# A new hand-written order for a cosine attention and highway FFN kernel: its first pair apart, whole-batch loads, one Newton chain per batch, and GpSimd operations marked to go ahead of VectorE

## The chip, the cores and the metric

The kernel runs on one core of one Trainium2 chip. The metric is device time in microseconds (us). Of the kernel before there are three runs: 308.99, 310.39 and 311.38 us, median 310.39. Engines are called by short names: PE (TensorE, matmuls), DVE (VectorE), ACT (ScalarE), POOL (GpSimd), SP (SyncE, which here only issues DMAs). A `q` behind a name (SPq, POOLq) is that engine's instruction queue.

## The reference, cut to what matters

```python
# q, k, v: (8, 12, 448, 64) float32; tau = 0.1; x: (3584, 768)
q_n = q / (np.linalg.norm(q, axis=-1, keepdims=True) + 1e-06)
k_n = k / (np.linalg.norm(k, axis=-1, keepdims=True) + 1e-06)
scores = np.matmul(q_n, k_n.transpose(0, 1, 3, 2)) / tau
attn = softmax(scores)                       # rows sum to 1
x = np.matmul(attn, v)                       # (8, 12, 448, 64)
x = x.transpose(0, 2, 1, 3).reshape(8 * 448, 12 * 64)
H = np.maximum(x @ w_h, 0.0)
T = 1.0 / (1.0 + np.exp(-(x @ w_t + b_t)))
out = T * H + (1.0 - T) * x                  # (3584, 768)
```

Eight batches of twelve heads: each head has 448 rows of 64. Then a two-matrix gated FFN over 3584 rows of 768.

## The kernel before, in words

**Tiling.** A batch has six *pairs*; pair p holds heads p and 6+p. The 448 rows of a head are three chunks of 128 ("main") and a tail of 64 ("tail"). With s = 6b + p, a pair goes through these steps:

- *Loads.* q and k main rows are cast to float16 by DMAs that POOL issues into `qr` and `kr` (`load_main`, L325 and on). The tails `qt` and `kt` and the values `vr` and `vt` come in float32 by DMAs that SP issues (`load_tails`, `load_v`). For batch 0, pairs 0 to 2 come in float32 into `f0` by SP (q) and ACT (k) instead (`load_first`), and its tails are spread over SP, POOL and ACT. From batch 2 on the loads are gated in the plan on an exponential of an earlier pair.
- *Norms.* Squares (L423 and L449 on ACT, L425 on DVE), two folding adds and a reduction on DVE (L440 to L442) give sums of squares `n2`. `newton` (L468 to L475) makes the reciprocal square root in seven small DVE instructions. A batch from 1 on has two such chains: tails with pairs 0 to 2 (48 columns), and pairs 3 to 5 (36 columns). Batch 0 has three: tails with pair 0, pairs 1 and 2, pairs 3 to 5.
- *Scaling.* `qn` and `kp` (L494) and the q tails `qtn` (L507) on POOL, 128x384 each, the k tails `kb` (L521) on DVE. For pair 0 of batch 0, `kp` is on DVE.
- *Turn.* Nine PE transposes into one PSUM bank (L539 to L547), copied by DVE to `qT` (L553).
- *Scores and exponentials.* Three chunks of scores (L562, two matmuls each) and one for the tails (L576); ACT takes exponentials of 128x896 into `E` (L569) and of 128x512 into `Et` (L581).
- *Attention.* 32 small PE matmuls of 65 columns (L610, L613, L629; the 65th column of the values is 1 and gives the row sum), then on DVE a reciprocal (L643) and a multiply into `x` (L646).

When a batch's six pairs are done its FFN follows, in four row tiles of 128 rows (the last one holds the 64 tail rows of two halves). The tile is transposed: for batches 1 to 6 by a DMA on SP (`xd`, L672), for batches 0 and 7 by PE and a DVE copy (L678, L683). Matmuls with `wt` and `wh` (L712, tails L707, bias L701 and L698) go to PSUM banks; ACT takes a tanh (L726), DVE makes `hm` (L733), the gate (L740) and their product (L744), POOL adds x (L750), SP stores (L758, L760). The last two tiles are added on DVE.

**What sets the order.** Nothing is scheduled at run time. Every step is recorded as an operation with an engine, reads, writes and a number in order of recording. `ORDER` lists these numbers; `pl.follow(ORDER, SLOTS)` (L814) replays them, and `SLOTS` names the buffer that each new tile takes. Each engine, and each engine's DMA queue, runs its own operations strictly in that order, waiting by semaphores for what it reads. An operation that is late therefore holds all that stand behind it on its engine. SP carries loads, transposes and stores in one queue.

[...]

The functions below are those of the kernel before, with the line numbers of its profile.

Of the kernel before, what the change touches and what calls it, by code (L numbers as in the profile page):

```python
# [15 lines left out]

ORDER = tuple(
    int(n)
    for n in """
# [83 lines left out]
22001023122030021300111011123110111101320111110002011122301023100123000200133222002110311220012011310010021300  # L103
20121013211220011301001231102110300011011021100231001120230022203001103112310222003121222130101102320103120201
22213
""".replace("\n", "")
)


# [10 lines left out]

class Plan:

    FREE = ("B", "sq", "f1", "f2")
    AHEAD = {"S": 2}
    SWITCH = 92.0
# [62 lines left out]
def pe(occ):  # L192
    return occ, occ + 205
# [665 lines left out]
```

## Time and profile before

| what | us |
|---|---|
| median of three runs | 310.39 |
| their range | 308.99 to 311.38 |
| the profiled execution, span from first to last instruction | 309.1 |
| PE busy in it | 266.1 |
| DVE busy | 236.1 |
| ACT busy | 206.4 |
| POOL busy | 149.7 |

The profile gives one execution and its span; it has no other time of its own, and the span lies between the lowest run and the median. In its rows L712 is line 712 of the kernel; `x4` is four instructions taken together; what stands in brackets is how long the engine was idle just before and what released it. Rows of stretches give, for each engine, busy us and in brackets the number of instructions, then the granted PE clock (1.00 is full), the busy share of the DMA engines and GB/s. A busy PE is not PE at its peak: a matmul's row includes its time in the pipeline.

### The profile page before, as it was taken

Reading aid. Unit: us, or ns where it says so; the run is one execution under the profiler, and the core shown is the slowest. Engines: PE = TensorE matmul, PEld = TensorE weight load, DVE = VectorE, ACT = ScalarE, POOL = GpSimd, SP = SyncE. Lnnn points to the kernel's source line nnn. Section 1 sums busy time; section 2 is a strip of 40 time slices with the busy share of each in tenths; the row PEclk is TensorE's granted clock in tenths of the full one; section 3 lists DMA queues with packets and bytes.
Section 4 is the critical chain, followed back from the end, with each engine's and each line's share of the span. In section 5 each row is a group of like instructions: output and inputs, shape, how many; then the busy total and the mean of one; then the engine's idle time right before and its main releaser. Section 6 shows DMA issues by size and latency. Waiting matters only on the chain.

```text
span 309.1 us, 7922 instructions
## 1 busy us (share of the span) xinstructions
PE 266.1 (86%) x3178; PEld 164.9 (53%) x3178; DVE 236.1 (76%) x548; ACT 206.4 (67%) x327; POOL 149.7 (48%) x162
## 2 busy tenths in 40 slices
PE   0039798999899999995699699989999999999992
PEld 0015566657565466554365556646666665656651
DVE  5798797798999659994689848996789855444574
ACT  1415799998897778761498368987498858771210
POOL 8244648416653862593432694429623780520440
PEclk9999799999999999999599899999999999999999
DMA  7999999993137794379815399714991221601223
GB/s 161 225 222 205 245 197 231 185 127 123 54 83 136 211 216 63 130 96 226 168 63 48 105 253 225 127 30 79 209 254 37 74 70 26 180 21 48 102 78 128
DMA packets 79749, 42.20 MB, mean 137 GB/s; under 512 B 60224, under 2 KB 76608, under 8 KB 79712
## 3 DMA queue, kind: packets, MB, share of 16 engines
q1 hardware_dynamic: 53104, 29.60, 40.5%
q0 software_dynamic: 24992, 11.31, 28.5%
q10 hardware_dynamic: 1616, 0.79, 1.0%
q8 instruction: 25, 0.41, 0.6%
q14 instruction: 12, 0.10, 0.1%
HBM read 37.75 MB, written 11.01 MB: 158 GB/s over the span
## 4 chain that ended last, share of the span: by engine, by line
PE 46%; DVE 22%; DMA 13%; issue 6%; SPq 5%; POOL 4%; ACT 2%; POOLq 0%; DVEq 0%; ACTq 0%
PE pB L712 20%; PE pS L562 6%; PE pB L613 5%; DMA kt<-in_k_dram 5%; DMA qr<-in_q_dram 3%; DMA qt<-in_q_dram 3%; DVE qT L553 2%; DVE sq L425 2%; PE pB L576 2%; DVE hm L733 2%; PE pB L707 2%; DVE x L646 2%; PE pB L610 2%; PE pB L629 2%; DVE n L442 2%
## 5 line engine op out<-in xcount | busy, mean ns | idle before, releaser
L569 ACT ACTIVATE E<-pS 128x896 f16<-128x896 f32 x144 | 126.5, 923 | 32.1 <-PE pS L562 31.6
L750 POOL TENSOR_TENSOR os<-x,hm 128x768 f32<-128x768 f16 (+1 forms) x30 | 44.3, 1484 | 63.7 <-DVE hm L744 45.7
L712 PEld LDWEIGHTS <-xT 128*128 128x128 f16 x576 | 52.5, 99 | 39.2 <-issue 11.3
L712 PE MATMUL pB<-wt,xT 128*128 128x384 f16 x288 | 61.5, 330 | 0.1
L712 PE MATMUL pB<-wh,xT 128*128 128x384 f16 x288 | 59.4, 328 | 0.7 <-DVE x L646 0.6
L613 PE MATMUL pB<-vp,E 128*128 128x65 f16 x864 | 49.5, 197 | 0.0
L494 POOL TENSOR_TENSOR kp<-kr,rs 128x384 f16<-128x384 f16 x45 | 37.0, 833 | 24.7 <-DVE sq L425 6.8
L562 PE MATMUL pS<-qT 64*128 64x448 f16 x288 | 45.5, 369 | 3.5 <-ACT E L569 2.3
L726 ACT ACTIVATE tt<-pB 128x384 f16<-128x384 f32 x56 | 27.7, 496 | 31.1 <-PE pB L712 26.0
L494 POOL TENSOR_TENSOR qn<-qr,rs 128x384 f16<-128x384 f16 x45 | 37.4, 843 | 19.6 <-DVE f L440 5.4
L610 PE MATMUL pB<-vp,Et 128*128 128x65 f16 x288 | 43.7, 196 | 1.5 <-DVE qT L553 0.9
L613 PEld LDWEIGHTS <-E 128*128 128x128 f16 x864 | 40.6, 100 | 4.1 <-issue 1.5
L733 DVE SCALAR_TENSOR_TENSOR hm<-pB,x 128x384 f16<-128x384 f32 x56 | 30.5, 551 | 14.8 <-PE pB L712 11.8
L581 ACT ACTIVATE Et<-pB 128x512 f16<-128x512 f32 x48 | 28.4, 605 | 14.3 <-PE pB L576 13.9
L553 DVE COPY qT<-pB 128x1024 f16<-128x1024 f16 x48 | 32.7, 685 | 5.7 <-PE pB L547 5.4
L610 PEld LDWEIGHTS <-Et 128*128 128x128 f16 x288 | 28.6, 99 | 8.7 <-issue 5.8
L646 DVE SCALAR_TENSOR_TENSOR x<-pB,rd 128x448 f16<-128x448 f32 x48 | 29.6, 621 | 0.9
L539 PE MATMUL pB<-ident,qtn 128*128 128x128 f16 x24 | 5.7, 236 | 22.9 <-POOL qtn L507 18.3
L562 PEld LDWEIGHTS <-qT 64*128 64x128 f16 x288 | 10.8, 94 | 25.1 <-issue 19.5
L643 DVE RECIPROCAL rd<-pB 128x7 f32<-128x7 f32 x48 | 9.2, 196 | 18.6 <-PE pB L613 18.2
L440 DVE TENSOR_TENSOR f<-sq 128x1152 f16<-128x1152 f16 (+2 forms) x25 | 15.6, 625 | 9.7 <-ACT sq L449 6.1
L507 POOL TENSOR_TENSOR qtn<-qt,rs 128x384 f16<-128x384 f32 x8 | 6.6, 828 | 31.8 <-DVE rs L475 27.4
(73 smaller groups left out, 453.9 us busy)
## 6 DMA issues: line engine op xcount, KB each, us to landing
vr<-in_v_dram SPq DMA_DIRECT2D x8, 1152.0 KB, 11.1
out_dram<-os SPq DMA_DIRECT2D x24, 384.0 KB, 2.7
kr<-in_k_dram POOLq DMA_DIRECT2D x7, 576.0 KB, 12.6
qr<-in_q_dram POOLq DMA_DIRECT2D x7, 576.0 KB, 9.7
vt<-in_v_dram SPq DMA_DIRECT2D x16, 96.0 KB, 8.5
out_dram<-os SPq DMA_DIRECT2D x16, 96.0 KB, 2.2
qt<-in_q_dram SPq DMA_DIRECT2D x30, 48.0 KB, 5.5
kt<-in_k_dram SPq DMA_DIRECT2D x14, 96.0 KB, 7.3
```

What stands on the lines that cost most here:

```text
L494: return e.tensor_mul(R("qn" if t == 0 else "kp", s).rearrange("l c ab d -> l ab c d"), rows(t, b, p, p + 1)[:, :, 0, :].rearrange("l ab ( ...
L553: op("DVE", f"cpT {s}", lambda: nc.vector.tensor_copy(R("qT", s)[:, :], R16(("T", ti))[:, :]), o, l, key, r=[("B", ("T", ti))], w=[("qT", s)])
L562: nc.tensor.matmul(R("S", 3 * s + c)[:, ab, 0:448], lhsT=qT[:, 512 + 128 * c : 640 + 128 * c], rhs=qT[:, 64 * (1 - ab) : 64 * (1 - ab) + 4 ...
L569: nc.scalar.activation(R("E", s)[:, c, :, 0:448], R("S", 3 * s + c)[:, :, 0:448], AF.Exp, scale=inv_tau)
L581: op("ACT", f"exp {s} t", lambda: nc.scalar.activation(R("Et", s)[:, 64:576], R("B", ("S", s))[:, :], AF.Exp, scale=inv_tau), o, l, key + 0.3,
L610: nc.tensor.matmul(U[:, 2 * c + ab, :], lhsT=Et[:, 128 + 128 * c : 256 + 128 * c], rhs=vp[:, 6 + ab, :], start=True, stop=False)
L613: nc.tensor.matmul(U[:, 2 * c + ab, :], lhsT=EF[:, j, 576 * ab + 128 * c : 576 * ab + 128 * c + 128], rhs=vp[:, 3 * ab + j, :], start=Fals ...
L646: op("DVE", f"ev {s}", lambda: nc.vector.scalar_tensor_tensor(out=R("x", b)[:, :, D * p : D * p + D], in0=U_()[:, :, 0:D], scalar=0.0, in1 ...
L712: nc.tensor.matmul(P[:, 0:MH], lhsT=xT[:, cc, :], rhs=w_[:, cc, MH * mh : MH * mh + MH], start=st, stop=(cc == CC - 1))
L726: op("ACT", f"th {g} {mh}", lambda pi=pi, mh=mh: nc.scalar.activation(R("tt", g)[:, MH * mh : MH * mh + MH], R("B", ("P", pi))[:, 0:MH], A ...
L733: nc.vector.scalar_tensor_tensor(out=R("hm", g)[:, MH * mh : MH * mh + MH], in0=R("B", ("P", pi))[:, 0:MH], scalar=0.0, in1=xs, op0=ALU.ma ...
L750: op(en, f"out {g}", lambda: eng.tensor_add(R("os", g)[:, 0:W], xall(), R("hm", g)[:, 0:W]), o, l, at + 0.1, r=[("gg", g), ("x", b)], w=[( ...
```

## The change

The arithmetic of the FFN, the scores and the attention is the same, and so are PE's 3178 matmuls that produce results. What differs:

- **First pair apart.** Only pair 0 of batch 0 comes in float32 (`f0`, q first on SP's queue, k first on ACT's). Its own tail rows are loaded apart from those of the other pairs (`load_first_tails`). `first_pair` squares them (q on DVE, k and tails on ACT), folds 15 columns, runs a Newton chain of 15 columns, and does all five scalings of the pair on DVE. Pairs 1 and 2, then 3 to 5, are loaded as float16 by POOL, in eight DMAs; their squares are all on ACT. The norm chains of batch 0 are then: pair 0; tails with pairs 1 and 2; pairs 3 to 5.
- **Whole-batch loads** from batch 1 on keep their shape, but every DMA is an operation of its own in the order (before, the DMAs of a tail or of two halves were recorded as one), and the gates are gone. The two DMAs of a tail tile's store, the clears of the buffers and the two halves of the v tail's copy are split too.
- **One Newton chain** for each of batches 2 to 7, over 84 columns (batch 1 keeps two). Newton steps and the v copies of batch 0 are now `port=True`.
- **Warm matmuls.** 20 operations of two matmuls each on a constant tile `fill`, results unused: eleven ahead of the first turn, nine later, among the pairs of batch 0.
- **Marked POOL operations.** 49 numbers in `URGENT`. In the replay a marked POOL operation makes the next DVE operation of the port wait for it, if no other POOL operation of the port stands between.
- **A new order** throughout, with new `SLOTS`.

On DVE the program has 499 rows where it had 538, on ACT 328 for 310, on SP 125 for 94 (DMAs of one line that stand together count once), on POOL 164 for 164. In the new order POOL issues the first loads, makes ten scalings of batch 0, and then issues the two weight loads; before, it issued the load of `wh` ahead of all scalings and that of `wt` among them.

The diff, cut to its core (the two tables of numbers, and steps that are only recorded apart, are left out):

```diff
+URGENT = frozenset(
+    int(n)
+    for n in """
+131 132 169 188 414 415 434 467 554 572 591 592 629 648 649 682 699 716 763 768 769 825 845 864 1003 1040 1041
+1078 1079 1112 1157 1217 1218 1237 1256 1294 1327 1361 1451 1452 1470 1542 1576 1587 1623 1628 1629 1648 1758
+""".split()
+)
...
+    fill = sb.tile([128, 384], FP16, name="fill")
+    f0 = sb.tile([128, 2, 2, NCH * D], FP32, name="first")
...
+    def warm(n, key):
+        i = fills[0]
+        fills[0] += 1
+
+        def fn():
+            for _ in range(n):
+                ins = nc.tensor.matmul(R("B", ("W", i))[:, 0:384], lhsT=fill[:, 0:128], rhs=fill[:, 0:384],
+                                       start=True, stop=True)
+            return ins
...
+    def load_first_tails(key):
+
+        for h, e, en in ((0, nc.sync, "SP"), (1, nc.sync, "SP")):
+            op(en, f"ldqa {h}", lambda h=h, e=e: e.dma_start(
+                R("qt", 0)[64 * h : 64 * h + 64, :, 0, :],
+                q[0, :, 3 * 128 : S, :].rearrange("(ab h) l d -> h l ab d", ab=2)[3 * h]), key, w=[("qt", 0, 0)])
+        for ab, e, en in ((0, nc.scalar, "ACT"), (1, nc.scalar, "ACT")):
+            op(en, f"ldka {ab}", lambda ab=ab, e=e: e.dma_start(
+                R("kt", 0)[64 * ab : 64 * ab + 64, 0, :], k[0, 6 * ab, 3 * 128 : S, :]), key + 0.01, w=[("kt", 0, 0)])
...
+    def first_pair(key):
+        def sqm(t):
+            d = sq0[:, 6 * t : 6 * t + 6, :].rearrange("l (a c) d -> l a (c d)", a=2)
+            a = f0[:, t]
+            return nc.scalar.activation(d, a, AF.Square) if t else nc.vector.tensor_mul(d, a, a)
...
+        steps("0 0", lambda: n20[:, :], lambda j: rs0[:, j, :], 15, [("n20", 0)], [("rs0", 0)], [], key + 0.1)
+        for t in range(2):
+            op("DVE", f"{'qk'[t]}n 0", lambda t=t: nc.vector.tensor_mul(
...
-            square(b, 0, 3, base - 5.0)
-            square_tail(b, base - 4.0)
-            newton(b, (6, 0, 1, 2), base - 3.9)
-            square(b, 3, 6, base - 2.5)
-            newton(b, (3, 4, 5), base - 2.4)
...
+            nb = base - (10 if b == 1 else 12)
+            square(b, 0, 3, nb)
+            square_tail(b, nb)
+            if b == 1:
+                newton(b, (6, 0, 1, 2), nb + 2)
+                square(b, 3, 6, nb + 4)
+                newton(b, (3, 4, 5), nb + 6)
             else:
+                square(b, 3, 6, nb - 3)
+                newton(b, (6, 0, 1, 2, 3, 4, 5), nb + 2)
...
-    last = None
+    last = ahead = None
     with nc.allow_low_precision(reason="fp16 operands of the products, squares and gates as given"):
         with tc.manual_schedule():
             for o in plan:
                 ins = o.fn()
                 if o.port and o.eng == "DVE":
-                    last = ins
-                elif o.port and last is not None:
-                    after(ins, last)
+                    if ahead is not None:
+                        after(ins, ahead)
+                    last, ahead = ins, None
+                elif o.port and o.eng == "POOL":
+                    if last is not None:
+                        after(ins, last)
+                    ahead = ins if o.seq in URGENT else None
```

More of the change, by code (lines that the diff above doesn't have):

```diff
@@ L276, in R16, with clear, fn @@
     def R16(i):
         return R("B", i).bitcast(FP16)
-    def clear(tiles, views):
-        def fn():
-            for t in tiles:
+    def clear(name, tiles, views, key, gap=0):
+        for n, t in enumerate(tiles):
+            def fn(t=t):
                 for vw, x in views(t):
-                    nc.vector.memset(vw, x)
-        return fn
-    def ident_():
-        make_identity(nc, ident)
+                    ins = nc.vector.memset(vw, x)
+                return ins
+            op("DVE", f"{name} {n}", fn, key + gap * n, w=[(name, n)])
@@ L304 @@
[L304 to L311 removed]
+        (t[0:64, :, 6, D : D + 1], 1.0), (t[64:128, :, 7, D : D + 1], 1.0)], 2, 22)
@@ L352, in load_tails, with fq @@
+    def load_tails(b, key):
         for h in range(2):
-            e, en = (nc.gpsimd, "POOL") if b == 0 and h == 1 else (nc.sync, "SP")
-            def fq(h=h, e=e):
-                for ab in range(2):
-                    e.dma_start(
+            for ab in range(2):
+                def fq(h=h, ab=ab):
+                    return nc.sync.dma_start(
                         R("qt", b)[64 * h : 64 * h + 64, ab],
-                        q[b, 6 * ab + 3 * h : 6 * ab + 3 * h + 3, 3 * 128 : S, :].rearrange("h l d -> l h d"),
-                    )
@@ new lines, in load_v, with weights @@
+    def load_v(b, key):
+        op("SP", f"ldv {b}", lambda: nc.sync.dma_start(R("vr", b)[:, :, :], main_src(v, b)), key, w=[("vr", b)])
+        for ab in range(2):
+            op("SP", f"ldvt {b} {ab}", lambda ab=ab: nc.sync.dma_start(
+                R("vt", b)[64 * ab : 64 * ab + 64, :, :], tail_src(v, b, ab)), key + 0.01, w=[("vt", b)])
+    def weights(key):
+        for w_src, w_dst, nm in ((moe_w_t, wt, "wt"), (moe_w_h, wh, "wh")):
+            op("POOL", f"ld {nm}", lambda w_src=w_src, w_dst=w_dst: nc.gpsimd.dma_start(
+                w_dst[:, :, :], w_src.rearrange("(cc p) m -> p cc m", p=128)), key, w=[(nm, 0)])
+        op("POOL", "ld b", lambda: nc.gpsimd.dma_start(bth[:1, :], moe_b_t), key, w=[("bth", 0)], r=[("zb", 0)])
@@ L412, in square, with fn @@
-    def square(b, p0, p1, key):
-        g0, g1 = 12 * (p0 % 3), 12 * (p0 % 3) + 12 * (p1 - p0)
-        n = 192 * 2 * (p1 - p0)
+        return ("qr" if t == 0 else "kr", b, p)
+    def square(b, p0, p1, key, engs=("DVE", "DVE")):
+        g1 = 12 * (p1 - p0)
         i = (b, p0)
-        for t in range(2):
-            onact = b == 0 and p0 < 3 and (p0 > 0 or t == 0)
-            def fn(t=t, onact=onact):
+        for t, eng in enumerate(engs):
+            def fn(t=t, eng=eng):
                 a = rows(t, b, p0, p1)
-                d = R("sq", i)[:, g0:g1, :].rearrange("l (p a c) d -> l a p (c d)", a=4, c=NCH)[:, 2 * t : 2 * t + 2]
-                if onact:
-                    nc.scalar.activation(d, a, AF.Square)
-                else:
-                    return nc.vector.tensor_mul(d, a, a)
-            o, l = act(n) if onact else dve(n, 1 if first(b, p0) else 2)
-            op("ACT" if onact else "DVE", f"sq {b} {p0} {t}", fn, o, l, key, r=[rowtok(t, b, p) for p in range(p0, p1)],
-               w=[("sq", i)], port=not onact)
-        folds(f"fold {b} {p0}", b, i, g0, g1, 12 + 12 * p0, [("n2", b, p) for p in range(p0, p1)], key)
@@ new lines, in fn, with folds, v_ @@
+                if eng == "ACT":
+                    return nc.scalar.activation(d, a, AF.Square)
+                return nc.vector.tensor_mul(d, a, a)
+            op(eng, f"sq{p1 - p0} {b} {p0} {t}", fn, key,
+               r=[rowtok(t, b, p) for p in range(p0, p1)], w=[("sq", i)], port=eng == "DVE")
+        folds(b, i, 0, g1, col(b, p0), [("n2", b, p) for p in range(p0, p1)], key)
+    def folds(b, i, g0, g1, to, done, key):
+        def v_(r):
+            return R(r, i)[:, g0:g1, :]
+        n = g1 - g0
+        w0, w1 = ("fa",) + i, ("fb",) + i
+        op("DVE", f"fa{n} {b} {i[1]}", lambda: nc.vector.tensor_add(v_("f1"), v_("sq")[:, :, 0:32], v_("sq")[:, :, 32:64]),
+           key, r=[("sq", i)], w=[w0], u=[("f1", i)], port=True)
+        op("DVE", f"fb{n} {b} {i[1]}", lambda: nc.vector.tensor_add(v_("f2"), v_("f1")[:, :, 0:16], v_("f1")[:, :, 16:32]),
+           key, r=[w0], w=[w1], u=[("f1", i), ("f2", i)], port=True)
+        op("DVE", f"fc{n} {b} {i[1]}", lambda: nc.vector.reduce_sum(R("n2", b)[:, to : to + n], v_("f2"), axis=AX.X),
+           key, r=[w1], w=done, u=[("f2", i), ("n2", b)])
@@ L463, in step, with steps @@
+    def steps(name, n2_, rs_, n, need, done, use, key):
         def step(i):
-            n2 = R("n2", b)[:, lo:hi]
-            y, t, u = (R("rs", b)[:, j, lo:hi] for j in range(3))
+            n2 = n2_()
+            y, t, u = (rs_(j) for j in range(3))
             v_ = nc.vector
             if i == 0:
-                v_.tensor_scalar(out=y.bitcast(I32), in0=n2.bitcast(I32), scalar1=-0.5,
-                                 scalar2=float(0x5F3759DF), op0=ALU.mult, op1=ALU.add)
-            elif i in (1, 4):
-                v_.tensor_mul(t, y, y)
-            elif i in (2, 5):
-                v_.scalar_tensor_tensor(out=u, in0=t, scalar=-0.5, in1=n2, op0=ALU.mult, op1=ALU.mult)
-            else:
-                v_.scalar_tensor_tensor(out=y, in0=u, scalar=1.5, in1=y, op0=ALU.add, op1=ALU.mult)
@@ new lines, in step @@
+            if i in (1, 4):
+                return v_.tensor_mul(t, y, y)
+            if i in (2, 5):
+                return v_.scalar_tensor_tensor(out=u, in0=t, scalar=-0.5, in1=n2, op0=ALU.mult, op1=ALU.mult)
+            return v_.scalar_tensor_tensor(out=y, in0=u, scalar=1.5, in1=y, op0=ALU.add, op1=ALU.mult)
+        for i in range(7):
+            op("DVE", f"nt{n} {name} {i}", lambda i=i: step(i), key + 0.001 * i,
+               r=need if i == 0 else [("nt", name, i - 1)], w=[("nt", name, i)] + (done if i == 6 else []), u=use, port=True)
@@ new lines, in ffn @@
+        rows_ = out[b * S : b * S + S]
+        if tail:
+            for h in range(2):
+                op("SP", f"sth {g} {h}", lambda h=h: nc.sync.dma_start(
+                    rows_[384:448, MH * h : MH * h + MH], R("os", g)[64 * h : 64 * h + 64, 0:MH]), at + 0.4,
+                   r=[("os", g)], w=[("o", g)])
+        else:
+            op("SP", f"st {g}", lambda: nc.sync.dma_start(
+                rows_[0:384].rearrange("(l c) m -> l c m", c=NCH)[:, i, :], R("os", g)[:, :]), at + 0.4,
+               r=[("os", g)], w=[("o", g)])
@@ new lines @@
+    OFF = 1.5
+    for b in range(B):
+        base = at_(6 * b)
+        if b == 0:
+            load_first(0)
+            load_first_tails(0.2)
+            load_main("qr", q, b, 1, 3, 1)
+            load_main("kr", k, b, 1, 3, 1.1)
+            load_main("qr", q, b, 3, 6, 4)
+            load_main("kr", k, b, 3, 6, 4.1)
+            load_v(b, 4)
+            weights(10)
+            first_pair(3)
+            square(b, 1, 3, 6, ("ACT", "ACT"))
+            square_tail(b, 6.5)
+            newton(b, (6, 1, 2), 7)
+            square(b, 3, 6, 10, ("ACT", "ACT"))
+            newton(b, (3, 4, 5), 11)
+            for n in range(20):
+                warm(2, 0.5 * n)
+        else:
+            ld = 8 if b == 1 else base - 40
+            load_main("qr", q, b, 0, 6, ld)
+            load_main("kr", k, b, 0, 6, ld + 0.1)
+            load_tails(b, ld + 4 if b == 1 else ld)
+            load_v(b, ld + 10)
+            nb = base - (10 if b == 1 else 12)
[5 more added lines that the diff above has]
+                newton(b, (3, 4, 5), nb + 6)
+            else:
+                square(b, 3, 6, nb - 3)
+                newton(b, (6, 0, 1, 2, 3, 4, 5), nb + 2)
+        qtnorm(b, base - 8 if b else 11)
+        ktnorm(b, base - 8 if b else 11)
+        vtcast(b, base - 6)
+        for p in range(NP):
+            s = 6 * b + p
+            t = at_(s)
+            if s > 0:
+                scaled(0, b, p, t - 6, "POOL")
+                scaled(1, b, p, t - 6, "POOL")
+            turn(b, p, t - 3)
+            vcast(b, p, t - 2)
+            scores(b, p, t)
+            attend(b, p, t + 3)
```

517 lines of the change are left out of this document (211 added, 306 removed), and 143 rows, old and new, of the table ORDER.

## The prediction

> **What bounds the kernel now.** I read the page first, then a table of busy time by stretch, then the timeline of the first 50 us, then the chain of waits and the DMA view.
>
> ```profile
> span 309.1 us, 7922 instructions
> ...
> PE 46%; DVE 22%; DMA 13%; issue 6%; SPq 5%; POOL 4%; ACT 2%; POOLq 0%; DVEq 0%; ACTq 0%
> ```
>
> The second line is the chain that ended last: PE holds less than half of it, so the end is set by PE with DVE steps and DMA landings between. Where PE sits still is seen in the stretches (PE busy first, then weight loads, DVE, ACT, POOL, granted clock, DMA share):
>
> ```profile
> 10.00:20.00 10.00, 1.14 (x9) 0.88 (x9) 8.56 (x26) 1.99 (x3) 3.01 (x4) 1.00 1.32 234
> 20.00:30.00 10.00, 8.01 (x64) 4.43 (x64) 8.45 (x22) 5.77 (x8) 4.98 (x6) 1.00 1.27 200
> 30.00:40.00 10.00, 7.70 (x97) 5.10 (x96) 8.10 (x21) 6.83 (x10) 6.38 (x8) 0.83 1.13 237
> 140.00:160.00 20.00, 14.54 (x176) 9.15 (x176) 11.40 (x23) 9.52 (x18) 7.92 (x9) 0.83 0.87 168
> 160.00:180.00 20.00, 17.53 (x200) 10.16 (x197) 17.01 (x42) 12.58 (x19) 9.31 (x12) 0.91 0.48 100
> 180.00:200.00 20.00, 20.00 (x250) 12.57 (x248) 16.21 (x32) 17.10 (x31) 10.97 (x11) 1.00 1.16 178
> 300.00:309.10 9.10, 3.30 (x33) 1.80 (x31) 4.93 (x10) 0.52 (x2) 0.76 (x1) 0.93 0.32 112
> ```
>
> A healthy stretch is 180 to 200: PE never idle, 250 matmuls in 20 us, or 12.5 per us. Against it stand four losses: the head (nothing before 10; 9 matmuls up to 20, 64 and 97 in the next two stretches), 5.46 us idle at 140 to 160, 2.47 at 160 to 180, and the 5.80 of the tail. The head and the middle are what the change can reach.
>
> The head, from the whole timeline and then from ACT's own:
>
> ```profile
> 3.22 1.55 POOL L334 DMA_DIRECT2D qr<-in_q_dram  x2
> ...
> 16.58 0.83 POOL L494 TENSOR_TENSOR qn<-f,rs 128x384 f16<-128x384 f32 x1 [3.24 <-DVE f L441]
> ...
> 18.26 0.29 PE L539 MATMUL pB<-ident,qtn 128*128 128x128 f16 x1 [18.26 <-POOL qtn L507]
> ```
>
> ```profile
> 21.67 0.60 ACT L581 ACTIVATE Et<-pB 128x512 f16<-128x512 f32 x1 [6.28 <-PE pB L576]
> 22.16 2.54 ACT L569 ACTIVATE E<-pS 128x896 f16<-128x896 f32 x3
> 24.57 1.06 ACT L597 CAST vp<-vt 64x384 f16<-64x384 f32 x2
> 26.83 1.96 ACT L569 ACTIVATE E<-pS 128x896 f16<-128x896 f32 x2 [1.20 <-PE pS L562]
> 30.96 0.52 ACT L449 ACTIVATE sq<-kt 128x384 f16<-128x384 f32 x1 [2.17 <-DMA kt<-in_k_dram]
> 31.39 3.32 ACT L569 ACTIVATE E<-pS 128x896 f16<-128x896 f32 x4
> ```
>
> ```profile
> 49.46 0.51 PE L678 MATMUL pB<-ident,x 128*128 128x128 f16 x6
> ```
>
> The first transposes wait for POOL, and POOL (qn, 16.58) waited 3.24 us for a fold of pairs 1 and 2 on DVE that pair 0 does not need. The first exponential comes at 21.67, and the first turn of attended rows (L678, the start of the FFN) at 49.46. Six pairs in 27.8 us is 4.6 each; ACT alone needs 3 x 0.83 + 0.60 = 3.09 for a pair.
>
> **The change part by part.** *Head.* Only pair 0 keeps the float32 path; its q goes first on SP's queue and its k first on ACT's, its 15 norm columns get a chain of their own, and its five scalings run on DVE, so the POOL wait of 3.24 is gone. But in the written order the fold and Newton steps of pairs 1 and 2 stand on DVE ahead of pair 0's tail scalings, and they read q and k of pairs 1 and 2, now loaded by POOL. The DMA view (size, median us to landing):
>
> ```profile
> wh<-in_moe_w_h_dram POOLq DMA_DIRECT2D x1, 1152.0 KB, 22.3
> wt<-in_moe_w_t_dram POOLq DMA_DIRECT2D x1, 1152.0 KB, 10.3
> f<-in_k_dram ACTq DMA_DIRECT2D x3, 192.0 KB, 5.4
> f<-in_q_dram SPq DMA_DIRECT2D x3, 192.0 KB, 6.2
> xT<-x SPq DMA_TRANSPOSE x24, 2.9
> qr<-in_q_dram POOLq DMA_DIRECT2D x2, 144.0 KB, 6.7
> kr<-in_k_dram POOLq DMA_DIRECT2D x2, 144.0 KB, 8.2
> kt<-in_k_dram ACTq DMA_DIRECT2D x2, 96.0 KB, 4.8
> ```
>
> POOL's issues take 1.55/2 = 0.78 each, so the fourth (k of pairs 1 and 2) goes at about 1.3 + 3 x 0.78 = 3.6 (estimate) and lands 8.2 later, at 11.8 (6.7 would give 10.3). ACT squares it (0.9 for 768 columns, by the 0.83 of an exponential of 896), then 14 DVE steps at 0.29 (mean of L473 below) follow: 11.8 + 0.9 + 4.1 = 16.8 for the first turn. From turn to first exponential before took 21.67 - 18.26 = 3.41, of which about 1 (estimate) is DVE doing a fold first; in the new order the copy is next on DVE, so 2.4, giving 19.2 against 21.67. From there ACT is the bound: six pairs at 3.09 = 18.5, plus 1.0 (estimate, 1152 columns) for a square of pairs 3 to 5 that moves from DVE to ACT, 2 x 0.52 for the squares of batch 1's tails and 1.06 for the v tail: 40.8, and 1.5 (estimate) for the last attention and its division: FFN starts at 42.3. Before, at 49.46, PE had also done 1.3 us of batch 1 (a turn and one pair's scores, 16 matmuls at 12.5 per us). Gain 49.46 - 1.3 - 42.3 = 5.9. I take 5.0, because the weights are now issued after ten POOL scalings, and a wait of 0.9 for them is likely. Ends: 0 (pair 0 held by loads as before) and 9 (the kt wait of 2.17, the shorter landing and faster steps on top).
>
> Of the two FFN weight loads, wh leaves POOL near 30 (ten scalings, of which the last wait for the second Newton chain), where before it went ahead of all scalings; its cover is the ACT-bound phase up to 42.3. Without it the price is under the rivals.
>
> *Forty warm matmuls.* 22 stand before turn 0, where PE did nothing, and the others between pairs that wait for ACT: cost 0, bounded by PE's idle 8.86 in 10 to 20. The gain: stretch 30 to 40 was granted 0.83, so PE was half-clocked in part; a warm clock shortens the first turn and scores by some 0.6. I take 0: the fills start when pair 0's q has landed and end near 12 (estimate), some 5 us before the turn. [...]
>
> *Loads on POOL's queue.* Eight pieces of batch 0 now go there. The row at 3.22 shows 0.78 for each issue beside a busy DVE. [...]
>
> *Later batches: loads.* What failed at 140 to 160, from the chain of waits:
>
> ```profile
> 137.36 0.71 SPq L357
> 138.11 8.47 DMA qt<-in_q_dram
> ```
>
> ```profile
> SPq L760 <- POOL os L750: 73.9, 18, 11.4
> ```
>
> The q tails were issued late on SP (behind stores that wait for POOL, second fence, 73.9 us in all), took 8.47 to land, ACT stood at the square, and DVE, POOL and PE after it. 8.47 us is 106 matmuls. In the order of before, of the tail loads of batches 2 to 7, 14 have fewer than 100 matmuls between issue and first reader (16 the fewest, those of the failing batch 37 to 61); in the new order 4 (61, 73, 76, 80). Of 5.46 idle I take 5.0 as gone (0.46 is ordinary). What is late next: k tails of batch 6 (61 matmuls, 4.9 us), which at a quiet landing is enough. Ends: 0 and 6.5 (the clock of 0.83 there too).
>
> *One Newton chain* for batches 2 to 7: 6 x 7 = 42 DVE instructions go; the others do 84 columns at about the same price.
>
> ```profile
> L471 DVE TENSOR_TENSOR rs<-rs 128x36 f32<-128x36 f32 (+2 forms) x34 | 13.5, 396 | 0.5
> L475 DVE SCALAR_TENSOR_TENSOR rs<-rs 128x36 f32<-128x36 f32 (+2 forms) x34 | 12.7, 374 | 0.6
> ...
> L473 DVE SCALAR_TENSOR_TENSOR rs<-rs,n 128x36 f32<-128x36 f32 (+2 forms) x34 | 9.9, 290 | 0.5
> ```
>
> Each chain has two of each and a seed: 2 x (0.396 + 0.374 + 0.290) = 2.12, times 6 = 12.7 us of DVE. With DVE at 22% of the chain, 2.8 of it is on the path. Ends 0 (all hidden) and 6 (half; the dip at 160 to 180, where DVE is busy 17 of 20, is such a place). Against it: all of batch b's pairs now wait for the later squares too; cover: in the new order the last Newton step stands some 5 us of PE's matmuls or more ahead of the first turn of its batch.
>
> [...]
>
> *New order, transposes by DMA.* They land in 2.9 (row above), 36 matmuls. With fewer than 50 matmuls ahead there were 2 of 24; now there are 9 (24 to 43). Three are short of 36, by up to 1 us each: 1.0 in all. Ends 0 and the rival below. PE's useful matmuls, the exponentials and the last tile on DVE are the same: tail 0.
>
> Sum against the profiled execution: 309.1 - 5.0 - 5.0 - 2.8 + 0.5 + 1.0 = 297.8. The median of the runs, 310.39, stands 1.3 above that execution, so **299.1**.
>
> **The rivals.** (1) *Slower: transposes take the place of the tail loads.*
>
> ```profile
> DMA to landing us min/median/max: 2.3/2.9/8.6
> ```
>
> Nine tiles have 24 to 43 matmuls, about 2.8 us, between issue and reader, and PE takes its work in order. Landing can be 8.6. If these nine land at a mean of 4.7 us, each stops PE for 1.8: 299.1 - 1.0 + 16.2 = 314.3. It decides (above 313.5) from a mean of 4.6. For it: SP carries loads, stores and transposes in one queue. Against: the median.
>
> (2) *The weights are late.* wt goes at about 29 (estimate: the second Newton chain ends near 24, and six scalings of 0.83 follow) and wh a little later. Landing like wt before (10.3) wt is there at 39, and PE does not wait; like wh before (22.3) it is there at 51 against 42.3, and PE, in order, waits 9. I take 5 between them: 304. For it: ten POOL scalings stand ahead. Against: when wh was issued before, most of the first loads were still outstanding.
>
> (3) *More is gained.* Landing 6.7 (-1.5), DVE steps at 0.2 (14 x -0.09, -1.3), Newton at half (-3.2), no transposes late (-1.0): 292.
>
> (4) The DVE time and the earlier head do not reach the end, because POOL and ACT take the place: only the stall goes, 299.1 + 5.0 + 2.8 = 306.9; I count it with (2).
>
> **How the numbers follow.** Forecast as summed 0.52 (own range 295 to 304), rival 1 0.20, rivals 2 and 4 0.15, rival 3 0.13. Within 1% (307.3 to 313.5, about what a measurement here can tell from no change) falls 0.02 of the forecast, 0.05 of rivals 2 and 4, 0.02 of rival 1; slower 0.18 of rival 1 and 0.01 of the rest; faster 0.72. The range 288 to 313 takes in the rest, with the end of the head's bound below rival 3, and leaves out most of rival 1.
>
> **What would show it.** Head: first exponential near 19.2, first transpose of attended rows near 42.3; wrong if the exponential is after 21.5 or PE waits for wt. Stall: no ACT wait over 3 us on a qt or kt DMA. Newton: 77 steps on DVE instead of 119 (34 + 34 + 34 and 17 seeds). Transposes: PE waits on xT of under 2 us in all; wrong if over 10.

## The result, and the profile after

The changed kernel takes 288.65 us (median of 4 runs, 288.05 to 290.73) against 310.15 for the kernel before: a ratio of 0.9326, 95% interval 0.9274 to 0.9378, or 21.5 us less. The forecast was 299.1, 11.3 below the median it started from; the result lies below the 295 to 304 given to the sum itself and 0.65 above the lower end of the whole range, 288 to 313. The profiled execution spans 286.3, 22.8 less than the 309.1 of before.

From the page of the kernel after: span, busy time of each engine, the chain that ended last.

```profile
span 286.3 us, 7983 instructions
...
PE 262.3 (92%) x3218; PEld 166.0 (58%) x3218; DVE 217.4 (76%) x509; ACT 208.4 (73%) x331; POOL 149.0 (52%) x163
...
PE 66%; DMA 11%; DVE 9%; ACT 8%; issue 2%; POOL 1%; SPq 1%; ACTq 0%; DVEq 0%
```

PE now holds 66% of the chain (46% before), DVE 9% (22%), SP's queue 1% (5%). The stretches that stood for before, and the first ten us (same columns):

```profile
0.00:10.00 10.00, 3.50 (x12) 1.61 (x13) 6.33 (x28) 2.99 (x5) 7.81 (x15) 1.00 1.03 154
10.00:20.00 10.00, 5.05 (x28) 2.38 (x26) 7.34 (x26) 3.52 (x7) 2.59 (x4) 0.85 1.33 240
20.00:30.00 10.00, 9.10 (x104) 5.29 (x103) 8.31 (x25) 9.95 (x14) 6.08 (x8) 0.98 1.22 223
30.00:40.00 10.00, 8.83 (x158) 6.03 (x154) 9.76 (x27) 9.97 (x16) 5.43 (x6) 1.00 1.15 177
140.00:160.00 20.00, 19.69 (x221) 11.72 (x215) 18.62 (x38) 14.98 (x25) 8.57 (x7) 1.00 1.13 180
160.00:180.00 20.00, 18.97 (x211) 12.60 (x212) 15.95 (x40) 12.60 (x26) 9.50 (x11) 1.00 0.66 169
280.00:286.30 6.30, 0.87 (x12) 0.35 (x8) 2.40 (x5) 0.48 (x1) 0.00 (x0) 0.75 0.29 95
```

In 20 to 40 ACT is busy 19.92 of 20 (12.60 before), and PE does 250 matmuls that produce results against 161 (the 262 of the rows hold twelve fill matmuls). The holes at 140 to 180 are gone, and with them the clock of 0.83 and 0.91 there. The tail keeps its idle time, 5.4 (5.8 before).

To see where the 22.8 come from I priced every matmul at its spacing where PE runs back to back at full clock (0.16 for 384 columns, 0.03 for 65, as L712 and L613 between 186 and 190 of the kernel before; the forty fill matmuls at nothing) and took "time less work": what PE has lost up to a mark. It is an estimate; a slightly different price of a matmul moves a piece by up to 0.7.

| mark, us | before | after | gained in the stretch |
|---|---|---|---|
| 60 | 34.8 | 28.1 | 6.7 |
| 120 | 41.4 | 34.4 | 0.3 |
| 140 | 43.6 | 35.1 | 1.5 |
| 160 | 52.2 | 36.1 | 7.6 |
| 180 | 57.4 | 37.6 | 3.7 |
| 240 | 62.5 | 40.3 | 2.4 |
| end | 70.0 | 47.2 | 0.6 |

So the head gives 6.7, the place of the stall 7.6, and some 8 come in pieces from 120 on. The marks are times, at which the kernel after has done more work; taken at equal work, the head gives 7.1, the stall 7.9 and the stretch to 180 4.7, so the picture stays. The head first, from the timelines of ACT and of PE in the kernel after:

```profile
19.30 0.60 ACT L580 ACTIVATE Et<-pB 128x512 f16<-128x512 f32 x1 [4.50 <-PE pB L577]
...
30.60 0.52 ACT L414 ACTIVATE sq<-kt 128x384 f16<-128x384 f32 x1
...
39.46 0.62 ACT L580 ACTIVATE Et<-pB 128x512 f16<-128x512 f32 x1
```

```profile
41.80 0.28 PE L663 MATMUL pB<-ident,x 128*128 128x128 f16 x2
...
43.39 1.15 PE L697 MATMUL pB<-wt,xT 128*128 128x384 f16 x6
```

The first exponential is at 19.30 (forecast 19.2, before 21.67), the first transpose of attended rows at 41.80 (42.3; before 49.46). No row of ACT between 19.30 and 40 carries a wait: the square of the k tails at 30.60, where before ACT waited 2.17, finds them there.

### The profile page after: what moved, and what is told of

It is laid out like the page before. It is cut to its first block, busy times and chain, and to the rows that moved or that the text cites. A ratio compares the mean times of both kernels' runs of the same rounds, so it can differ in the third digit from the quotient of the medians.

```text
span 286.3 us, 7983 instructions
## 1 busy us (share of the span) xinstructions
PE 262.3 (92%) x3218; PEld 166.0 (58%) x3218; DVE 217.4 (76%) x509; ACT 208.4 (73%) x331; POOL 149.0 (52%) x163
## 4 chain that ended last, share of the span: by engine, by line
PE 66%; DMA 11%; DVE 9%; ACT 8%; issue 2%; POOL 1%; SPq 1%; ACTq 0%; DVEq 0%
PE pB L697 26%; PE pS L564 9%; PE pB L610 7%; DMA xT<-x 5%; PE pB L692 5%; ACT E L571 5%; PE pB L626 3%; PE pB L577 3%; PE pB L607 3%; DMA qr<-in_q_dram 3%; PE pB L686 2%; PE pB L547 2%; PE pB L543 2%; DMA kt<-in_k_dram 2%; DVE x L636 2%
## 5 line engine op out<-in xcount | busy, mean ns | idle before, releaser
L571 ACT ACTIVATE E<-pS 128x896 f16<-128x896 f32 x144 | 126.4, 922 | 22.9 <-PE pS L564 19.2
L697 PE MATMUL pB<-wt,xT 128*128 128x384 f16 x288 | 59.9, 326 | 2.1 <-DMA xT<-x 2.1
L697 PE MATMUL pB<-wh,xT 128*128 128x384 f16 x288 | 57.9, 326 | 0.8 <-DVE sq L391 0.8
L499 POOL TENSOR_TENSOR kp<-kr,rs 128x384 f16<-128x384 f16 x47 | 38.5, 828 | 27.0 <-DVE rs L440 9.4
L499 POOL TENSOR_TENSOR qn<-qr,rs 128x384 f16<-128x384 f16 x47 | 38.8, 830 | 21.5 <-issue 3.6
L607 PE MATMUL pB<-vp,Et 128*128 128x65 f16 x288 | 43.1, 193 | 1.7 <-DVE tt L725 1.3
L564 PE MATMUL pS<-qT 64*128 64x448 f16 x288 | 42.5, 356 | 1.4 <-ACT E L571 0.9
L610 PEld LDWEIGHTS <-E 128*128 128x128 f16 x864 | 39.5, 98 | 3.1
L607 PEld LDWEIGHTS <-Et 128*128 128x128 f16 x288 | 28.1, 98 | 9.7 <-issue 5.9
L725 DVE TENSOR_SCALAR tt<-tt 128x768 f16<-128x768 f16 (+1 forms) x32 | 13.8, 432 | 9.6 <-POOL os L733 7.4
L588 ACT CAST vp<-vr 128x384 f16<-128x384 f32 x42 | 21.0, 518 | 0.1
L577 PE MATMUL pB<-qT 128*128 128x512 f16 x48 | 18.2, 385 | 0.2
```

Source lines behind the costliest of these rows:

```text
L499: return e.tensor_mul(R("qn" if t == 0 else "kp", s).rearrange("l c ab d -> l ab c d"), rows(t, b, p, p + 1)[:, :, 0, :].rearrange("l ab ( ...
L564: ins = nc.tensor.matmul(R("S", 3 * s + c)[:, ab, 0:448], lhsT=qT[:, 512 + 128 * c : 640 + 128 * c], rhs=qT[:, 64 * (1 - ab) : 64 * (1 - a ...
L571: return nc.scalar.activation(R("E", s)[:, c, :, 0:448], R("S", 3 * s + c)[:, :, 0:448], AF.Exp, scale=inv_tau)
L607: nc.tensor.matmul(U[:, 2 * c + ab, :], lhsT=Et[:, 128 + 128 * c : 256 + 128 * c], rhs=vp[:, 6 + ab, :], start=True, stop=False)
L610: ins = nc.tensor.matmul(U[:, 2 * c + ab, :], lhsT=EF[:, j, 576 * ab + 128 * c : 576 * ab + 128 * c + 128], rhs=vp[:, 3 * ab + j, :], star ...
L697: ins = nc.tensor.matmul(P[:, 0:MH], lhsT=xT[:, cc, :], rhs=w_[:, cc, MH * mh : MH * mh + MH], start=st, stop=(cc == CC - 1))
```

## The experiments

Each was timed beside the kernel before, on one chip for each group: median 310.11 beside the tail loads, the two chains, the marks and the fills; 311.15 beside batch 5 early, batches 3 to 7 early and the two experiments on `port`; 311.32 beside the other four. Ratios are to that kernel before. The kernels are named as "before, with" or "after, with" an edit. Numbers in the diffs are entries of ORDER. `port` is a flag of the program: in the replay each POOL operation with `port=True` waits for the last DVE operation with it that stands ahead. In the kernel before, the Newton steps and the v copies of batch 0 are without it.

**Only the tail loads early** (before; 1114, 1113 are the q tails of batch 5, 1115 its k tails, 434 the store of tile 5):

```diff
-... 784 621 434 912 ... 933 1114 1112 ... 1111 819 1115 821 ... 925 1113 926
+... 784 621 1114 1115 1113 434 912 ... 933 1112 ... 1111 819 821 ... 925 926
```

> The kernel before, with only the q and k tail loads of batch 5 moved ahead of three stores on SP's queue. Theory: these loads alone made the stall at 138 to 154; issued some 8 us earlier they are there when ACT squares them, so the ACT wait of 6.4 goes, and with it the half clock of 147.4 to 154.2. That is 5.0 of idle time and half of 6.8, 8.4 in all: 302 against 310.2, with the dip at 170 to 178 still there. Rival 1: q and k of the same batch hold the chain too (q landed at 147.27, as late as the tails), and less than 2 is won: 308 to 310. Rival 2: the dip at 170 to 178 is a child of the stall and goes as well (2.5 of idle, 1.7 of clock): 298.

Measured: 310.41 (six runs: one of 304.12, which stands alone and isn't explained, and five of 309.73 to 312.46, the profiled one among them). In these five nothing is gained, though ACT's wait is gone, as rival 1 has it. Its stretch, and the timelines of DVE and POOL there:

```profile
140.00:150.00 10.00, 5.97 (x87) 4.06 (x86) 4.90 (x11) 3.47 (x6) 4.17 (x6) 0.83 1.33 181
```

```profile
146.22 0.76 DVE L425 TENSOR_TENSOR sq<-kr 128x1152 f16<-128x1152 f16 x1 [3.94 <-DMA kr<-in_k_dram]
```

```profile
133.05 1.08 POOL L329 DMA_DIRECT2D kr<-in_k_dram  x1
```

PE still stands for 4 us and drops to half clock: 0.83 granted over the row, and three transposes take 0.53 at 147.56 against 0.33 at 139.11. DVE now waits 3.94 for k of the same batch, which POOL issued at 133.05 and which DVE gets 13.2 later. The stall had a second wait right behind the first.

**All q and k loads of batch 5 early** (before; 1111, 1112 are the whole-batch q and k on POOL's queue):

```diff
-... 752 447 934 ... 762 766 763 453 920 ... 457 906
+... 752 1114 1112 447 934 ... 762 766 1111 763 453 1115 920 ... 457 1113 906
```

> The kernel before, with all q and k loads of batch 5 (the two whole-batch loads on GpSimd's queue and the tails on SP's) 14 us of TensorE work earlier. Theory, new after the tails alone did nothing: the stall has two waits one behind the other, ACT for the tails and then DVE for the k of the batch (3.94 in that run). With both gone the 5.0 of idle and half of the 6.8 at half clock go: 310.1 - 8.4 = 302, and no DVE wait on k or q of that batch is over 1. Rival: the Newton chain that stands beside GpSimd operations at 136 to 141 (steps of 0.75 to 1.57) holds the same place, and half stays: 306.

Measured: 303.85, ratio 0.977 (0.9714 to 0.9825): 7.3 gained, near the 8.4 of the theory. Its stretch:

```profile
140.00:150.00 10.00, 10.00 (x154) 6.69 (x151) 8.42 (x18) 7.25 (x13) 5.68 (x7) 1.00 0.27 75
```

The whole-batch loads alone were not moved. That the tails would then still have held the stretch is read from ACT's timeline of the kernel before:

```profile
146.68 0.52 ACT L449 ACTIVATE sq<-qt 128x384 f16<-128x384 f32 x1 [6.41 <-DMA qt<-in_q_dram]
```

**All q and k loads of batches 3 to 7 early** (before; the same for 25 entries, here the whole-batch loads 895, 896 of batch 4):

```diff
-... 413 422 895 610 ... 898 425 896 722
+... 582 535 895 547 ... 214 600 896 602
```

> The kernel before, with all q and k loads of batches 3 to 7 14 us of TensorE work earlier. Theory: only batch 5 was late, so the result is that of batch 5 alone, 302. Rival 1: short leads cost in every batch (GpSimd's loads had 8 to 14 us of TensorE work between issue and first reader and took 8 to 13 to land), and it is 298 or less. Rival 2: loads that come earlier collide with the transposes by DMA of the batch before, and the gain is given back: over 305.

Measured: 312.47, ratio 1.0043 (1.0011 to 1.0076): the gain is given back, as rival 2 has it. From the timelines of POOL, SP and PE:

```profile
86.85 1.07 POOL L329 DMA_DIRECT2D qr<-in_q_dram  x1
```

```profile
91.09 6.80 SPq L672 DMA_TRANSPOSE xT<-x  x3
```

```profile
99.64 1.14 PE L712 MATMUL pB<-wt,xT 128*128 128x384 f16 x3 [6.92 <-DMA xT<-x]
```

The whole-batch loads of batch 4 now go out at 86.85 and 87.91, just ahead of the first DMA transposes at 91.09. PE waits 6.92 for the first of these, which lands 8.5 after its issue. Time less work grows by 8.2 between 80 and 100 (by 1.8 in the kernel before). The loads of five batches moved at once, so that these two loads make the loss is read from the trace. Here a load had to be early, but not just ahead of a transpose.

**The loads of batch 5 late again** (after; 1160 and 1161 are its whole-batch q and k, and its six tail loads move as well):

```diff
-... 667 702 1160 968 ... 568 741 1161 479
+... 979 689 1160 854 ... 817 827 1161 981
```

> The changed kernel with the q and k loads of batch 5 as late as before the change: the whole-batch loads some 8 us of TensorE work ahead of their first reader, the tails some 5. Theory: the stall comes back (ACT or DVE waits several us for one of these loads, TensorE stands and then runs at half clock) and costs the 7.3 that it brought in the kernel before: 296. Rival: the changed kernel has slack at that place and takes it in, 2 at most: 289 to 291.

Measured: 295.25, ratio 0.9507 (0.9454 to 0.956): 6.6 above the changed kernel, or some 5.6 by the two ratios. The size is near that of the theory, the place mostly not. From the timelines of PE and ACT:

```profile
118.22 1.80 PE L697 MATMUL pB<-wt,xT 128*128 128x384 f16 x6 [3.79 <-DMA xT<-x]
```

```profile
162.57 0.52 ACT L414 ACTIVATE sq<-qt 128x384 f16<-128x384 f32 x1 [2.76 <-DMA qt<-in_q_dram]
```

The late k load went out at 109.45, amid the transposes of batch 2: two that took 2.8 and 2.9 to land now take 8.4 and 7.7, and 3.3 more are lost in 100 to 120. The waits of the late loads' own readers (2.76 on ACT, 2.28 on DVE) cost about 1. So it shows that these loads can be issued at a bad time, and not that the old stall comes back.

**Two Newton chains again** (after):

```diff
+            if n < 84:
+                return part(i, 0, n)
+            part(i, 0, 48)
+            return part(i, 48, n)
```

> The changed kernel with each Newton step of batches 2 to 7 as two instructions (48 and 36 columns), so 42 DVE instructions more in the same places. Theory, as predicted: DVE has 42 more steps at 0.2, 8.4 us, of which some 22 to 30 per cent show: 288.7 + 2.2 = 290.9. Rival 1: DVE is off the path there and the time stays, 288.7 +- 1. Rival 2: longer chains meet GpSimd operations again, steps take 0.4, and it costs 6 or more.

Measured: 289.42, ratio 0.931 (0.9254 to 0.9366): the same time, as rival 1 has it. DVE's busy time is 218.7 against 217.4.

**No marks** (after; URGENT is empty):

```diff
-131 132 169 188 ... 1629 1648 1758
```

> The changed kernel with no GpSimd operation marked, so VectorE never waits for one. Theory: the marks neither cost nor bring anything that can be measured, 288.7 +- 1.4, and the mean of a Newton step of later batches stays near 0.25. Rival: the marks are what keeps the Newton steps from standing beside a GpSimd scaling; without them their mean goes back to 0.35 or more, as before, and the time rises by 3 to 6, to 292 to 295.

Measured: 289.29, ratio 0.9301 (0.9245 to 0.9357). No difference; the means of the steps of later batches stay at 0.23 to 0.25 (0.26 for the first step of a chain).

**Newton steps without `port`** (after):

```diff
-... (done if i == 6 else []), u=use, port=True)
+... (done if i == 6 else []), u=use)
```

> The changed kernel with its Newton steps no longer counted among the operations that GpSimd waits for. Theory: their mean goes up from 0.25 to 0.30 or more, as before, DVE's busy time rises by 3 to 8, and the time by about 3: 292. Rival: the new order keeps the two apart by itself, and the time stays at 288.7 +- 1.

Measured: 288.48, ratio 0.9264 (0.9224 to 0.9304). The same time; the rival holds. The means are 0.22 to 0.28.

**Newton steps with `port`** (before; each step also returns its instruction):

```diff
-... if i == 6 else []), u=[("rs", b), ("n2", b)])
+... if i == 6 else []), u=[("rs", b), ("n2", b)], port=True)
```

> The kernel before, with its Newton steps counted among the operations that GpSimd's scalings and sums wait for, and nothing else. Theory: a step beside a GpSimd operation lasts as long as that operation (0.75 against 0.20), so the mean of the steps falls from 0.29 to 0.40 down to 0.25 or less, DVE's busy time falls by 12 or more of 236.1, and the dip at 170 to 178 (2.5 of idle, 1.7 of clock) goes: 305 to 306. Rival: GpSimd waits as long as DVE did, its scalings come later, and the time stays at 310 or rises to 313.

Measured: 312.38, ratio 1.0011 (0.9976 to 1.0046). No gain; the rival holds. The steps did change in part: the mean of L475's falls from 374 to 223 ns, that of L471's stays at 390, 15 of the 119 steps still take over 0.5 (25 before), and DVE's busy time falls by 5.6 only.

**A chain behind a copy** (before, on top of batch 5's early loads; 1140 to 1144 are steps 0 to 4 of its second chain, 1014 is the copy of pair 28):

```diff
-... 1140 1152 1013 1141 1142 839 1143 988 1144 987 1151 1014 1006 1007 1145
+... 1152 1013 839 988 987 1151 1014 1006 1007 1140 1141 1142 1143 1144 1145
```

> The kernel before with all q and k loads of batch 5 early, and besides with five steps of the second Newton chain of that batch put behind the copy of pair 28's transposes instead of ahead of it, on DVE. Theory: in that kernel four steps of this chain lasted 0.71 to 0.83 beside GpSimd's scalings, the copy stood behind them, TensorE waited 2.48 for it and ran at half clock for 3.4 after it. With the copy ahead, 2.48 + 1.7 go: 303.9 - 4.2 = 299.7. Rival: the chain meets GpSimd one place later, what stands behind it then (the division and the next copy) waits as long, and the time stays at 303 to 304.

Measured: 305.68, ratio 0.9852 (0.9784 to 0.992), not below the 303.85. The rival holds; from PE's timeline:

```profile
168.01 0.38 PE L576 MATMUL pB<-qT 128*128 128x512 f16 x1 [2.68 <-DVE x L646]
```

The wait for the copy (2.48) has become a wait for the division behind the chain, of 2.68.

**Pair 0's scalings ahead of the folds** (before; 67 and 63 are pair 0's scalings on POOL, 41 the first fold of pairs 1 and 2):

```diff
-... 18 64 41 51 42 43 67 44 45 63 251
+... 18 64 67 63 41 51 42 43 44 45 251
```

> The kernel before with pair 0's two GpSimd scalings written ahead of the folds of pairs 1 and 2, so that they no longer wait for the second of these folds on DVE (3.24). Theory, as the prediction had the head: the first turn and the first exponential come 2.4 earlier (about 15.9 and 19.3), and the time falls by as much, 310.5 to 308. Rival: pairs 1 and 2 are no earlier, since their own scalings still wait for the second Newton chain, ACT waits for them instead, and less than 1 reaches the end: 309.5 to 311.

Measured: 312.55, ratio 1.0022 (0.9973 to 1.0072). POOL's wait falls from 3.24 to 0.96 and the first turn comes at 15.49, 2.8 earlier, but the first exponential at 20.74, only 0.93 earlier, and the end not at all. From DVE's timeline:

```profile
14.66 1.38 DVE L425 TENSOR_TENSOR sq<-qr 128x1152 f16<-128x1152 f16 x1
...
16.93 0.18 DVE L468 TENSOR_SCALAR rs<-n 128x24 int32<-128x24 int32 x1
...
18.68 0.76 DVE L440 TENSOR_TENSOR f<-sq 128x1152 f16<-128x1152 f16 x1
19.36 0.68 DVE L553 COPY qT<-pB 128x1024 f16<-128x1024 f16 x1
```

The copy of the turned rows has no wait of its own: it stands in DVE's order behind the squares, folds and Newton steps of pairs 1 to 5.

**First turn earlier** (after; 57 to 59 are pair 0's tail scalings on DVE):

```diff
-... 55 102 67 1 105 62 ... 58 73 74 57 75 59 76
+... 55 102 57 58 59 67 1 105 62 ... 72 73 74 75 76
```

> The changed kernel with pair 0's three tail scalings on DVE ahead of the tails' folds of pairs 1 and 2 instead of amid their Newton chain. Theory: the first turn comes at 12.6 instead of 16.8 and the first exponential at about 15.2; but the scalings of pair 1 still wait for the second chain (GpSimd at 17.4), so ACT is idle after pair 0 and only 1 to 2 of the 4 reach the end: 287. Rival: none of it reaches the end, 288.5 +- 1, since ACT has its squares to do in that time in either order.

Measured: 288.27, ratio 0.9301 (0.9239 to 0.9363), the same as the changed kernel within the intervals. The turn is at 12.61, but the scores wait until 18.15, from PE's part of the timeline:

```profile
12.67 0.33 PE L543 MATMUL pB<-ident,qn 128*128 128x128 f16 x3
...
18.15 0.39 PE L577 MATMUL pB<-qT 128*128 128x512 f16 x1 [4.55 <-DVE qT L553]
```

Again it is the copy, which I had left behind the chain. A version with the copy moved too was not run.

**Fill matmuls cut to 8 columns** (after):

```diff
-... [:, 0:384], lhsT=fill[:, 0:128], rhs=fill[:, 0:384],
+... [:, 0:8], lhsT=fill[:, 0:128], rhs=fill[:, 0:8],
```

> The changed kernel with the forty warm matmuls cut from 384 columns to 8, so that they keep TensorE busy for almost nothing. Theory: they bring nothing, since the clock is half at the first turn with them too; the first turn of attended rows stays within 0.5 of 41.8, time 288.7 +- 1. Rival: the fills between the pairs hold the clock up until the FFN starts; without them the clock falls to half again between 20 and 42, the FFN starts 2 us later or more, and the time is 291 or more.

Measured: 289.54, ratio 0.9313 (0.9262 to 0.9364): no difference. Three transposes of the first turn and of the second, from PE's timeline of the kernel after, then of this one:

```profile
16.86 0.47 PE L543 MATMUL pB<-ident,qn 128*128 128x128 f16 x3
...
20.77 0.33 PE L543 MATMUL pB<-ident,qn 128*128 128x128 f16 x3
```

```profile
16.99 0.52 PE L543 MATMUL pB<-ident,qn 128*128 128x128 f16 x3
...
20.58 0.53 PE L543 MATMUL pB<-ident,qn 128*128 128x128 f16 x3
```

The mechanism of the rival is there, its price is not. With the fills the second turn is warm (0.33); without them three transposes still take 0.53 at 25.03, and the first matmuls with `wt` start at 44.03 instead of 43.39. These 0.64 are too little to be told in the time.

## Why the prediction was right in sign and half in size

*Head: forecast 5.0, measured 6.7.* Both landmarks came within 0.5, and the first turn at the 16.8 of the sum, but in part by luck. From the DMA view of the kernel after:

```profile
wt<-in_moe_w_t_dram POOLq DMA_DIRECT2D x1, 1152.0 KB, 10.1
...
qr<-in_q_dram POOLq DMA_DIRECT2D x2, 96.0 KB, 4.6
...
kr<-in_k_dram POOLq DMA_DIRECT2D x2, 96.0 KB, 5.0
```

The pieces of pairs 1 and 2 (96 KB) landed in 4.6 and 5.0 instead of the 8.2, which was the time of the larger pieces of pairs 3 to 5. k was there at 8.4 and not at 11.8. What ACT waited for was a load that the sum did not hold, the k tails of the other pairs:

```profile
11.98 0.52 ACT L414 ACTIVATE sq<-kt 128x384 f16<-128x384 f32 x1 [3.44 <-DMA kt<-in_k_dram]
```

They landed at 11.96, by chance where the sum had put k. Behind them the squares took 1.7 instead of 0.9, and DVE's steps up to the turn 3.15 instead of 4.1. It is also the one wait of ACT over 3 on a tail load, which the prediction had as a sign of being wrong, though it had it for the stall.

wt, issued at 30.9, was there at 41.0, ahead of its reader at 43.39, so the 0.9 set aside for it was not needed and rival 2 was wrong there. The reading that POOL's wait of 3.24 made the head late fails as it stands: taken away alone it moves the first turn by 2.8, the first exponential by 0.93 and the end by nothing, since the copy behind the turn stands late in DVE's order. In the trace the gain is that ACT, once started, never waits. Which parts of the new head make that so was not isolated.

*Fill matmuls: forecast 0, measured 0; the reason given covers the first turn.* With them the first turn ran as cold as without (0.47 and 0.52 for three transposes), 4.8 after the last fill; in the experiment with the first turn earlier it stands right behind the last fill and took 0.33. Shorter holes cost the clock too: 2.47 of idle in the kernel before (up to 174.43; 0.50 granted from 175 to 178) and 2.48 with batch 5 early (up to 165.53; 0.64 in 164 to 168, 0.94 in 168 to 172) were each followed by 3.4 at half clock. That a gap of some 5 would lose the warmth was the author's estimate. The 0.6 named for a warm first turn and scores is near what the kernel after shows: a turn takes 1.06 at 16.80 and 0.67 at 20.71, the tail scores 0.61 at 18.65 and 0.39 at 23.71. The fills between the pairs did keep PE warm from the second turn on (0.33; 0.53 without them). That this gave no more than the 0.64 above fits with ACT, busy 19.92 of 20, as the bound of that stretch.

*Loads on POOL's queue.* All eight pieces landed in 4.4 to 5.8, beside a DVE busy 6.33 in the first 10, so no price of the move shows in these rows. Up to 6.4 nearly all of DVE's work is clears of buffers; pieces beside other DVE work were not measured apart.

*Stall: forecast 5.0, measured 7.3 (batch 5 early) and 7.6 in its stretch.* Two steps failed. The tails that "took 8.47 to land", with ACT at the square and "DVE, POOL and PE after it", are the first of two waits; the second is k of the same batch, on POOL's queue, whose loads the working hadn't counted. Taking away the first alone gave nothing in five runs of six. And "Of 5.46 idle I take 5.0 as gone" left out what follows the idle: the 0.83 in that row is (1 - 0.83) x 20 = 3.4 us lost to half clock (0.50 granted from 147.4 to 154.2). The row was quoted, and only the upper end had it. What the prediction named as late next in the new order, the k tails of batch 6, did come late, and cost little (PE's idle time is 0.31 in 140 to 160 and 1.03 in 160 to 180). From ACT's timeline of the kernel after:

```profile
159.11 0.52 ACT L414 ACTIVATE sq<-kt 128x384 f16<-128x384 f32 x1 [2.15 <-DMA kt<-in_k_dram]
```

*Newton: forecast 2.8; for the number of steps, nothing that can be told was measured.* The price of a step was mis-sized. From the view of tile rs of the kernel before (min/median/max in ns):

```profile
L471 DVE TENSOR_TENSOR rs<-rs x34: 107/206/1090, 10.6 to 235.5; 128x36 f32<-128x36 f32 x16, 128x48 f32<-128x48 f32 x14, 128x24 f32<-128x24 f32 x4
L473 DVE SCALAR_TENSOR_TENSOR rs<-rs,n x34: 176/198/1577, 10.8 to 235.7; 128x36 f32<-128x36 f32 x16, 128x48 f32<-128x48 f32 x14, 128x24 f32<-128x24 f32 x4
```

Half of all steps take 0.2 or less; the means of 0.29 to 0.40 in the prediction come from 25 of 119 steps over 0.5, which hold 22.1 of 41.1 us. Over nine tenths of each of these lie beside one POOL operation, and most last about as long as it does. From the groups of the kernel after:

```profile
L437 DVE TENSOR_TENSOR rs<-rs 128x84 f32<-128x84 f32 (+2 forms) x20 | 5.1, 257 | 0.4
L440 DVE SCALAR_TENSOR_TENSOR rs<-rs 128x84 f32<-128x84 f32 (+2 forms) x20 | 4.8, 241 | 0.4
L439 DVE SCALAR_TENSOR_TENSOR rs<-rs,n 128x84 f32<-128x84 f32 (+2 forms) x20 | 4.8, 239 | 0.3
```

Wider steps, yet near 0.24, because only 4 of 77 are over 0.5. DVE's busy time fell by 18.7, more than the 12.7 counted, but splitting the chains again costs 1.3 of it: the fall comes from where the steps now stand, not from their number. One place where the long steps of before stood ahead of PE is the dip at 160 to 180, from DVE's timeline:

```profile
172.16 0.75 DVE L475 SCALAR_TENSOR_TENSOR rs<-rs 128x36 f32<-128x36 f32 x1
172.95 0.83 DVE L471 TENSOR_TENSOR rs<-rs 128x36 f32<-128x36 f32 x1
```

Four such steps in a row (0.71 to 0.83), the copy of a turn behind them, and PE idle for 2.47 until it came. The kernel after has no such row there and gains 3.7 in that stretch. That the one makes the other is not shown: with the chain put behind the copy the wait only moved.

*Marks: forecast +0.5, measured 0.* Neither the marks nor `port` on the Newton steps is needed to keep the steps apart: without either one the time and the means stay (289.29 and 288.48; 0.22 to 0.28). So it is the written order, by elimination; a kernel without both was not run. No run shows the 0.5 that the sum took for the marks: without them the time is the same.

*Transposes by DMA: forecast +1.0.* PE's and its weight loads' waits in the kernel after:

```profile
PEld L697 <- DMA xT<-x: 3.6, 3, 1.6
...
PE pB L697 <- DMA xT<-x: 2.1, 2, 1.2
```

2.1 on PE, where before had no such row, and just over the 2 that the prediction allowed. Rival 1 did not come, but its mechanism is real: two of the experiments met it, at 6.9 and 3.8. The time lies nearest to rival 3 (292), though not by its terms.

*What the sum did not hold.* Some 8 us after 120, outside the stall (1.5, 3.7, 2.4, 0.6). The 3.7 is the dip above: 2.47 of idle and (1 - 0.91) x 20 = 1.8 of clock. DVE's lower load fits, but neither the flag `port` nor one moved chain brought any of it to the order of before, so its cause stays open beyond "the new order as a whole".

## What to carry to other kernels

When a stall is to be removed, look for the second wait behind the first, in every queue that feeds that stage, and price the cold clock after the hole together with the hole: here 3.4 us beside 5.46 of idle. A mean duration of a short step may come from a few long ones, here 25 of 119, most beside a POOL operation: read its median beside it before multiplying. Issuing loads early gave 7.3 for batch 5 alone and nothing for batches 3 to 7, where a DMA transpose went out close behind two of them and PE waited 6.92. A landmark that comes on time does not prove the path to it: look which wait ended last there.

## What the runs showed of the hardware

A DMA transpose that lands in 2.8 in a quiet stretch takes far longer when a whole-batch load of 576 KB was issued shortly before it: 8.5 and 8.4 in the two experiments. In the kernel after, seven of 24 take 6.0 or more, and each goes out at most 2.6 after a whole-batch load: five after one of q or k on POOL's queue (6.5 to 8.8), two after one of v, 1152 KB, on SP's own (6.7 and 6.0). The other 17 land in 2.3 to 4.5. From its view of tile xT:

```profile
DMA to landing us min/median/max: 2.3/3.0/8.8
```

In the kernel before, a Newton step of 0.20 takes 0.75 beside a POOL scaling of 0.83. And the granted clock of a row doesn't always show a cold start. In the kernel after it does: 0.85 in 10 to 20, with three transposes at 0.47. But with the fills cut, this stretch has 1.00 while three transposes in it took 0.52 instead of 0.33:

```profile
10.00:20.00 10.00, 2.33 (x16) 1.43 (x16) 6.95 (x24) 3.33 (x7) 2.47 (x4) 1.00 1.31 237
```
